# Reordered front of a convolution and MLP kernel: due times, one table half on GpSimd, and index fields as array operations

## The chip, the cores and the metric

The kernel runs on one core of one Trainium2 chip. The metric is the device time of one execution, in microseconds (us). A core has five instruction queues that matter here: TensorE (PE, with its weight loads as PEld), VectorE (DVE), ScalarE (ACT), GpSimd (POOL) and SyncE (SP). Each runs its instructions in program order and waits at semaphores. SP and POOL also issue the DMA transfers, which 16 DMA engines carry out.

## The reference

Inputs are bfloat16, with S = 2048 positions, D = 448 channels and F = 1792 hidden units. `q` is both the input and the residual.

```python
def _A_ref(q, k, v, shift_k, ssm_k, ssm_D):      # q is the layer-normed input
    for t in range(4):                            # four-tap causal filter of k
        k_shift = k_shift + k_pad[:, t:t + S, :] * shift_k[:, 3 - t][None, None, :]
    kv = k_shift * v
    # long causal convolution of kv with ssm_k over S, by FFT of length 2*S
    y = irfft(rfft(kv) * rfft(ssm_k))[:S] + kv * ssm_D
    return q * y

x = A_q
h = x + _A_ref(_layernorm(x), A_k, A_v, A_shift_k, A_ssm_k, A_ssm_D)
# token-mixing MLP on the layer-normed layernorm of h, then a residual
u = gelu(einsum("bsd,sf->bdf", layernorm(layernorm(h)), w1) + b1)
h2 = h + transpose(einsum("bdf,fs->bds", u, w2) + b2)
```

So the work has two halves: a long convolution, done as a discrete Fourier transform of `kv` (called u in the kernel) and of the filter `ssm_k` (called k), and a two-layer MLP across positions.

## The kernel before

**Layout.** Position s = 16 q + r lies in partition q and row r (R = 16 rows of 448 channels).

**The transform** has two stages in each direction. *Stage 1* (`emit_stage1`) multiplies each row r of k or u with two 128 x 128 tables E[2r], E[2r+1] on TensorE into a pair of PSUM banks (L935; for row 0 of k, L939 adds the `ssm_D` term). A *ring copy* (L945) takes the 128 x 896 result to one of eight ring slots in SBUF, and two DMAs (L949) shuffle it into TK (for k) or TU (for u): 112 partitions through POOL's queue, 16 through SP's. Every row goes to partitions that all second-stage products need, so *stage 2* (`emit_stage2`, L966, copies by `evac` at L652 to L656) can begin only when all 16 rows of a branch have landed. Stage 2 uses a small table FW. The *inverse* (`emit_products_i1`) multiplies the two spectra on VectorE (L1017), applies the small tables MA, MN, MB (L1029), copies into TU, and shuffles (L1039) into TZ. `emit_i2` then does the last inverse stage (L1105), the gate (L1112), the residual product (L1119) and the layer norms. The MLP follows (L1200, L1210, L1220, L1224).

**Before stage 1.** The filter is loaded (L810) and transposed on TensorE into KT (`emit_kT`, L916, eight copies by `evac`), between warm-up matmuls (`dummy`, L906). For u, `emit_kv` spreads the four taps over the partitions (WT, four matmuls L870 and four copies), multiplies on VectorE each row's four shifted rows by the taps (L881, 16 times), sums them on TensorE (L887) and multiplies by v (L890, eight times, two rows each). These are the *tap products*. Row r reads rows r to r+3 of KH, whose first three are the *halo* (L822, L824), loaded after the four chunks of k (L818) and of v (L827). The loads of x (L840) and of the first half of w1 (L1175) wait for the last u shuffle; the loads of w2 (L1185) and the second half of w1 (L1178) wait for the last inverse shuffle.

**Tables.** `emit_tables` makes E in two halves of eight rows each: an integer product (L753), an addition (L758) and a mask (L761) per half, then two sines on ScalarE (L766). For FW, MA, MB and MN, integer fields of the partition index are taken into columns of `pc` (L729 to L740, cast at L747), go through POOL (L773, L777), VectorE (L779, masks at L785) and a sine (L781) to POOL's products (L790, L793). `emit_ct` reorders E on POOL (L987, L992) and transposes it into ET (L998).

**The order.** Nothing of the order is written by hand. `op()` records each operation with what it reads and writes, the engine or engines that may do it, an estimated duration, and a due time `sch.t0`. `_Sched.schedule()` is a list scheduler: at each moment it gives a free engine the ready operation with the smallest due time (a longer remaining path breaks ties), and never leaves an engine idle while it has something ready. Readiness goes by the estimates, so the order in which instructions stand in an engine's queue is fixed when the kernel is built. The constants T_... in `_build` are the due times: T_K1 and T_DK1 for stage 1 of k, T_U1 for u, T_KV for the tap products, T_K2 and T_U2 for stage 2, T_TH for the second half of E, T_TN for the fields and small tables, T_CP and T_CT for ET, T_Q and T_DQ for the statistics of x, T_I2 and T_M1 for the end.

An operation with two engines, `FX = ("act", "dve")`, is *flexible*. VectorE takes one only if ScalarE will be busy for at least `flex_slack` ns more, or has at least `flex_back` operations ready:

```python
if (e == "dve" and len(ops[oid].engs) > 1 and
        free_at["act"] - t < self.flex_slack and not self.backlog(ready, ops, started, ready_t, t)):
```

Of the kernel before, what the change touches and what calls it, by code (L numbers as in the profile page):

```python
# [7 lines left out]
ALU = mybir.AluOpType  # L8
# [90 lines left out]
class _Sched:  # L99
# [137 lines left out]

    flex_slack = 200.0
    flex_back = 4

# [269 lines left out]
def _build(nc, A_q, A_k, A_v, A_shift_k, A_ssm_k, A_ssm_D, B_w1, B_b1, B_w2, B_b2, out):  # L510
# [5 lines left out]
    Bsz, S, D = A_q.shape  # L516
# [10 lines left out]
    i32 = DT.int32  # L527
# [38 lines left out]
    with ctx:  # L566
        sch = _Sched(nc, ctx, n_dma_sems=112, small_off=SMALL)
        op = sch.op
# [4 lines left out]
        def view(off, shape, dtype=bf16):  # L573
            size = 4 if dtype in (f32, i32) else 2
            n = 1
            for s_ in shape:
                n *= s_
            ap = AR[:, off // 2: off // 2 + n * size // 2]
            if dtype is not bf16:
                ap = ap.bitcast(dtype)  # L580
            if len(shape) == 2:
                ap = ap.rearrange("p (a b) -> p a b", b=shape[1])
            elif len(shape) == 3:
                ap = ap.rearrange("p (a b c) -> p a b c", b=shape[1], c=shape[2])
            return ap
# [32 lines left out]
        def small(nb):  # L618
            o = sm["o"]
            sm["o"] = o + nb  # L620
            assert sm["o"] <= TOT
            return o

        psum = _Pool(8, pairs=True)
# [13 lines left out]
        FX = ("act", "dve")  # L638
        T_KV, T_DKV, T_KT, T_K1, T_DK1, T_U1, T_DU1 = -7.65, 1.291, -30.53, -12.02, 4.106, 22.58, 2.723
        T_K2, T_U2, T_D2, T_CT, T_BIAS, T_I1, T_DI1 = 38.0, 41.07, 0.276, 40.65, 56.3, 33.93, 0.974  # L640
        T_Q, T_DQ, T_I2, T_DI2, T_M1, T_W1 = 63.71, 8.969, 80.2, 0.401, 96.28, 120.92

        T_TH, T_TN = -43.26, 2.34
        T_CP, T_XL, T_WB = 44.55, -25.02, 149.54
        N_WZ, N_WI, N_W0, N_WK = 24, 16, 9, 5
# [15 lines left out]
        def emit_tables():  # L661
# [27 lines left out]
            assert o_gc + 2560 + 4 * NB <= o_TT + 16384  # L689
            sch.t0 = 0.0  # L690
            op("pool", lambda e, W: e.iota(srow, [[1, R]], base=0, channel_multiplier=R), w=[(o_s, 64)])
# [9 lines left out]
            sch.t0 = 1.0  # L701
            sch.t0 = -30.0
            op("pool", lambda e, W: e.iota(idi, [[1, 128]], base=0, channel_multiplier=-1), w=[(o_gc + 1024, 512)],
               n=128, kind="iota")
            sch.t0 = 1.0
            op("pool", lambda e, W: e.iota(pc[:, 0:1], [[0, 1]], base=0, channel_multiplier=1), w=[(o_p, 4)])
            op("pool", lambda e, W: e.iota(gcol, [[0, 8], [512, 16]], base=0, channel_multiplier=0), w=[(o_gc, 512)],
# [19 lines left out]

            def ints(dst, src, a, b=None):
                op("dve", lambda e, W: e.tensor_scalar(  # L729
                    out=pc[:, dst:dst + 1], in0=pc[:, src:src + 1], scalar1=a[1], scalar2=b[1] if b else None,  # L730
                    op0=a[0], **({"op1": b[0]} if b else {})), r=[(o_p + 4 * src, 4)], w=[(o_p + 4 * dst, 4)], n=1)
            SHR, SHL, AND = ALU.logical_shift_right, ALU.logical_shift_left, ALU.bitwise_and

            sch.t0 = T_TN
            ints(1, 0, (SHR, 6))
            ints(2, 0, (AND, 32), (SHR, 4))
            ints(3, 0, (AND, 3), (SHL, 2))
            op("dve", lambda e, W: e.tensor_tensor(out=pc[:, 1:2], in0=pc[:, 1:2], in1=pc[:, 2:3], op=ALU.bitwise_or),
               r=[(o_p + 4, 8)], w=[(o_p + 4, 4)], n=1)
            op("dve", lambda e, W: e.tensor_tensor(out=pc[:, 4:5], in0=pc[:, 1:2], in1=pc[:, 3:4], op=ALU.bitwise_or),  # L740
               r=[(o_p + 4, 12)], w=[(o_p + 16, 4)], n=1)
            ints(5, 0, (AND, 16), (SHL, 7))
            ints(6, 0, (SHR, 2), (AND, 3))
            ints(7, 0, (AND, 15))
            ints(8, 0, (AND, 15))
            ints(9, 0, (SHR, 4), (AND, 3))
            op("dve", lambda e, W: e.tensor_copy(out=pcf[:, 0:6], in_=pc[:, 4:10]), r=[(o_p + 16, 24)],  # L747
               w=[(o_p + 48, 24)], n=6)
            for h in range(2):
                sch.t0 = T_TH if h else -40.0  # L750
                o_ph = (o_pi, o_X)[h]
                ph = view(o_ph, [16, 128], i32)
                op("dve", lambda e, W, h=h, ph=ph: e.tensor_tensor(  # L753
                    out=ph[:, :, 64:128].rearrange("p (r x) f -> p r x f", x=2),
                    in0=frow.rearrange("p (x f) -> p x f", x=2).unsqueeze(1).broadcast_to([128, 8, 2, 64]),
                    in1=srow[:, 8 * h:8 * h + 8].unsqueeze(2).unsqueeze(3).broadcast_to([128, 8, 2, 64]), op=ALU.mult),
                   r=[(o_fr, 512), (o_s, 64)], w=[(o_ph, 8192)], n=HALF, kind="1x")
                op("dve", lambda e, W, ph=ph: e.tensor_scalar(  # L758
                    out=ph[:, :, 0:64], in0=ph[:, :, 64:128], scalar1=2048, scalar2=None, op0=ALU.add),
# [105 lines left out]
        def emit_kv():  # L865
            sch.t0 = 3.5
            op("pool", lambda e, W: e.memset(ONE, 1.0), w=[(o_one, 256)], n=128)
# [60 lines left out]
        def emit_stage1(src, o_src, T, o_T, tag):  # L928
            for r in range(R):
# [13 lines left out]
                def fn(e, W, b=b, w=w):  # L943
                    dst = WR(w.slots[0])
                    return e.copy(out=dst, in_=Ppair(b)) if W == "act" else e.tensor_copy(out=dst, in_=Ppair(b))  # L945
                op(FX, fn, br=[b], bw=[w], n=2 * D, kind="psum")
                p0 = 64 * (r & 1) + 32 * ((r >> 1) & 1) + (r >> 2)
# [332 lines left out]
```

## Time and profile before

| what | value |
|---|---|
| median of 13 runs | 192.52 us (190.46 to 194.94) |
| the profiled execution | 193.02 us, span 191.2 us |
| PE busy | 175.5 us, 92% of the span |
| DVE busy | 112.1 us, 59% |
| ACT busy | 96.1 us, 50% |
| POOL busy | 68.8 us, 36% |
| mean granted TensorE clock | 0.973 |
| moved by DMA | 35.42 MB, mean 185 GB/s |

The span runs from the first to the last instruction of the profiled execution. A line of the *timeline* or of the *chain of waits* begins with start and duration in us; engine, line of the kernel, operation and tiles follow; brackets hold how long the engine sat idle before it and what released it. A line of the *groups* gives all instructions of one line and shape: their number after the x, then total busy us and mean ns, then idle time before them. All of SBUF is one tile, `arena`, and all of PSUM is `ps`, so instructions are best told apart by their lines.

### The profile page before, as it was taken

The numbers are of one execution on the slowest core, as the hardware profiler recorded it, in microseconds if no ns is written. First come the engines' busy times: TensorE is split into PE (matmuls) and PEld (weight loads), VectorE is DVE, ScalarE is ACT, GpSimd is POOL, SyncE is SP. The second block draws the span as 40 slices with busy tenths as digits, with TensorE's granted clock in tenths as the row PEclk, the third lists the DMA queues.
The fourth block names the chain that finished last, engine by engine and source line by source line (L and its number), as shares of the span: only waits on it lengthen the run. The fifth ranks groups of instructions, "written<-read, shape, count | busy, mean of one in ns | idle before, by whom it ended". The sixth has DMA issues, their size and how long they took to land.

```text
span 191.2 us, 2813 instructions
## 1 busy us (share of the span) xinstructions
PE 175.5 (92%) x1031; PEld 92.9 (49%) x1031; DVE 112.1 (59%) x185; ACT 96.1 (50%) x141; POOL 68.8 (36%) x162
## 2 busy tenths in 40 slices
PE   7899899988498898899789999999999999999993
PEld 2751444334253333224234444555556777777772
DVE  7781989979779999899788875100000222122221
ACT  3095789697969898981479846171221000000000
POOL 8033796669740024449476786000000000000000
PEclk9995799999969999999999999999999999999999
DMA  5996457998664999866599999300000011111111
GB/s 159 409 418 243 139 162 207 221 241 201 154 181 120 392 385 369 275 202 205 159 416 420 419 407 405 111 0 0 0 0 3 8 40 48 48 51 48 48 48 48
DMA packets 15723, 35.42 MB, mean 185 GB/s; under 512 B 3869, under 2 KB 9886, under 8 KB 15710
## 3 DMA queue, kind: packets, MB, share of 16 engines
q1 hardware_dynamic: 11102, 25.59, 35.9%
q0 software_dynamic: 4608, 9.66, 18.2%
q8 instruction: 8, 0.13, 0.3%
q14 instruction: 5, 0.04, 0.1%
HBM read 22.37 MB, written 1.84 MB: 127 GB/s over the span
## 4 chain that ended last, share of the span: by engine, by line
PE 68%; ACT 12%; DMA 9%; DVE 4%; POOL 3%; issue 2%; SPq 1%; ACTq 0%; POOLq 0%
PE ps L1220 22%; PE ps L1210 11%; PE ps L1200 10%; DMA arena<-arena 6%; ACT arena L652 5%; PE ps L966 4%; ACT arena L945 4%; PE ps L1105 4%; PE ps L1029 4%; PE ps L935 3%; DMA arena<-in_A_ssm_k_dram 3%; PE ps L887 2%; ACT arena L1112 2%; PE ps L916 2%; DVE arena L1017 2%
## 5 line engine op out<-in xcount | busy, mean ns | idle before, releaser
L1224 DVE SCALAR_TENSOR_TENSOR arena<-ps,arena 128x448 bf16<-128x448 f32 x16 | 10.9, 684 | 57.3 <-PE ps L1220 57.3
L1220 PE MATMUL ps<-arena 128*128 128x448 bf16 x224 | 42.5, 352 | 0.0
L1220 PEld LDWEIGHTS ps<-arena 128*128 128x128 bf16 x224 | 32.3, 144 | 10.1
L945 ACT CAST arena<-ps 128x896 bf16<-128x896 f32 x29 | 24.9, 914 | 6.5 <-PE ps L939 2.0
L652 ACT CAST arena<-ps 128x896 bf16<-128x896 f32 (+2 forms) x32 | 24.9, 862 | 1.7 <-PE ps L966 0.9
L1200 PE MATMUL ps<-arena 128*128 128x448 bf16 x112 | 23.0, 352 | 0.0
L949 POOL DMA_DIRECT2D arena<-arena x32 | 19.2, 601 | 8.5 <-ACT arena L945 6.6
L1210 PE MATMUL ps<-arena 128*128 128x448 bf16 x112 | 21.4, 352 | 0.0
L935 PE MATMUL ps<-arena 128*128 128x448 bf16 x64 | 17.7, 388 | 1.7 <-DVE arena L890 0.8
L1190 ACT ACTIVATE arena<-ps,arena 128x448 bf16<-128x448 f32 x14 | 8.2, 639 | 20.2 <-PE ps L1210 14.7
L966 PE MATMUL ps<-arena 128*64 128x448 bf16 x128 | 15.9, 390 | 2.6 <-POOL arena L992 1.6
L881 DVE TENSOR_TENSOR arena<-arena 128x1792 bf16<-128x1792 bf16 x16 | 17.9, 1161 | 0.0
L1039 POOL DMA_DIRECT2D arena<-arena x16 | 9.4, 593 | 23.3 <-ACT arena L652 23.1
L1112 ACT ACTIVATE arena<-ps,arena 128x448 f32<-128x448 f32 x16 | 11.5, 723 | 11.2 <-PE ps L1105 8.4
L1017 DVE TENSOR_TENSOR arena<-arena 128x1792 bf16<-128x1792 bf16 x16 | 16.4, 1085 | 0.0
L1029 PE MATMUL ps<-arena 64*128 64x448 bf16 x128 | 14.2, 352 | 2.4 <-ACT arena L652 1.5
L887 PE MATMUL ps<-arena 128*128 128x448 bf16 x64 | 14.4, 353 | 1.8 <-ACT arena L945 1.7
L1200 PEld LDWEIGHTS ps<-arena 128*128 128x128 bf16 x112 | 10.9, 98 | 10.2 <-DVE arena L1160 0.2
L1210 PEld LDWEIGHTS ps<-arena 128*128 128x128 bf16 x112 | 11.0, 98 | 10.2
L1119 DVE SCALAR_TENSOR_TENSOR arena<-arena 128x448 f32<-128x448 bf16 x16 | 10.8, 681 | 4.6 <-ACT arena L1112 4.3
L966 PEld LDWEIGHTS ps<-arena 128*64 128x64 f16 x128 | 6.9, 117 | 11.1 <-ACT arena L652 2.8
L1105 PE MATMUL ps<-arena 128*128 128x448 bf16 x32 | 8.7, 357 | 2.1 <-DMA arena<-arena 1.4
(85 smaller groups left out, 193.9 us busy)
## 6 DMA issues: line engine op xcount, KB each, us to landing
arena<-arena POOLq DMA_DIRECT2D x48, 196.0 KB, 5.2
arena<-in_B_w_dram SPq DMA_DIRECT2D x8, 896.0 KB, 14.1
arena<-in_B_w_dram SPq DMA_DIRECT2D x2, 2048.0 KB, 9.9
arena<-in_B_w_dram SPq DMA_DIRECT2D x2, 1536.0 KB, 17.7
arena<-in_A_k_dram SPq DMA_DIRECT2D x4, 448.0 KB, 8.4
arena<-in_A_v_dram SPq DMA_DIRECT2D x4, 448.0 KB, 9.0
arena<-in_A_q_dram SPq DMA_DIRECT2D x4, 448.0 KB, 4.7
out_dram<-arena SPq DMA_DIRECT2D x7, 224.0 KB, 1.9
```

Source lines behind the costliest of these rows:

```text
L652: return e.copy(out=dst(), in_=src())
L881: op("dve", lambda e, W, T=T, i=i, r=r: e.tensor_tensor(out=T[:, i], in0=KH[:, r:r + 4, :], in1=WT, op=ALU.mult), r=[(o_KH + r * DB, 4 * D ...
L887: op("pe", lambda e, W, b=b, T=T, i=i, j=j: e.matmul(Pb(b, i), ID, T[:, i, j, :], start=(j == 0), stop=(j == 3)), r=[(o_ID, 256), (o + (i ...
L935: op("pe", lambda e, W, b=b, r=r, h=h, dl=dl: e.matmul(Pb(b, h), E[:, 2 * r + h, :], src[:, r, :], start=True, stop=not dl), r=[r_E(r), (o ...
L945: return e.copy(out=dst, in_=Ppair(b)) if W == "act" else e.tensor_copy(out=dst, in_=Ppair(b))
L949: shuf[tag + q_ + str(r)] = shuf[tag + q_] = op(q_, lambda e, W, w=w, p0=p0, a=a, b_=b_, j0=j0: e.dma_start(T[p0:p0 + 29:4, j0:j0 + (b_ - ...
L966: op("pe", lambda e, W, b=bs[h], h=h, j=j, c=c, par=par: e.matmul(PS[64 * par:64 * par + 64, b.slots[c], 0:D], FW[:, 64 * c:64 * c + 64], ...
L1017: op("dve", lambda e, W, m=m, i=i: e.tensor_tensor(out=MR(m.slots[0]).rearrange("p (x y) d -> p x y d", x=2), in0=TU[:, i].unsqueeze(2).br ...
L1029: k = op("pe", lambda e, W, b=bs[h], m=ms[h], par=par, t=t, tab=tab, xy=xy, P=P: e.matmul(Pb(b, par), tab[P, :], MR(m.slots[0])[P, xy, :], ...
L1200: op("pe", lambda e, W, r=r, fc=fc, b=bs[fc]: e.matmul(Pb(b), W1A[:, r, 128 * fc:128 * fc + 128], Q[:, r, :], start=(r == 0), stop=(r == R ...
L1210: op("pe", lambda e, W, r=r, fc=fc, b=b: e.matmul(Pb(b), W1B[:, r, 128 * (fc - n0):128 * (fc - n0) + 128], Q[:, r, :], start=(r == 0), sto ...
L1220: op("pe", lambda e, W, r=r, fc=fc, b=b: e.matmul(Pb(b), W2[fc // 7][:, fc % 7, r:S:R], G[:, fc, :], start=(fc == 0), stop=(fc == NFC - 1) ...
```

## The change

- Due times: stage 1 of k goes from -12.02 + 4.106 r to -39.56 + 0.55 r, the tap products from -7.65 to -37.75, stage 1 of u from 22.58 to 0, stage 2 of u from 41.07 to 9.62 and of k from 38.0 to 29.29 (u now before k), the inverse's products from 33.93 to 12.82, the small tables from 2.34 to -30, and others as the diff shows.
- Ring copies of stage 1 (L945) may go to ScalarE only.
- The product and the addition of E's second half go to POOL; its mask stays on VectorE.
- The fields of the partition index are taken by one array shift, one array AND and two ORs, on a ramp with step 128, with shift counts and masks that 16 POOL memsets write.
- `flex_slack` goes from 200 to 600 and `flex_back` from 4 to 2.

```diff
-    flex_slack = 200.0
-    flex_back = 4
+    flex_slack = 600.0
+    flex_back = 2
...
-        T_KV, T_DKV, T_KT, T_K1, T_DK1, T_U1, T_DU1 = -7.65, 1.291, -30.53, -12.02, 4.106, 22.58, 2.723
-        T_K2, T_U2, T_D2, T_CT, T_BIAS, T_I1, T_DI1 = 38.0, 41.07, 0.276, 40.65, 56.3, 33.93, 0.974
-        T_Q, T_DQ, T_I2, T_DI2, T_M1, T_W1 = 63.71, 8.969, 80.2, 0.401, 96.28, 120.92
-
-        T_TH, T_TN = -43.26, 2.34
-        T_CP, T_XL, T_WB = 44.55, -25.02, 149.54
+        T_KV, T_DKV, T_KT, T_K1, T_DK1, T_U1, T_DU1 = -37.75, 0.96, -43.81, -39.56, 0.55, 0.0, 0.9
+        T_K2, T_U2, T_D2, T_CT, T_BIAS, T_I1, T_DI1 = 29.29, 9.62, 1.375, 22.37, 56.3, 12.82, 0.974
+        T_Q, T_DQ, T_I2, T_DI2, T_M1, T_W1 = 83.98, 17.938, 85.76, 0.401, 91.84, 122.45
+
+        T_TH, T_TN = -38.0, -30.0
+        T_CP, T_XL, T_WB = 20.0, -37.92, 154.44
...
-            sch.t0 = 0.0
+            sch.t0 = -70.0
             op("pool", lambda e, W: e.iota(srow, [[1, R]], base=0, channel_multiplier=R), w=[(o_s, 64)])
...
-            sch.t0 = -30.0
+            sch.t0 = -69.0
             op("pool", lambda e, W: e.iota(idi, [[1, 128]], base=0, channel_multiplier=-1), w=[(o_gc + 1024, 512)],
...
-            op("pool", lambda e, W: e.iota(pc[:, 0:1], [[0, 1]], base=0, channel_multiplier=1), w=[(o_p, 4)])
+            op("pool", lambda e, W: e.iota(pc[:, 0:1], [[0, 1]], base=0, channel_multiplier=128), w=[(o_p, 4)])
...
             sch.t0 = T_TN
-            ints(1, 0, (SHR, 6))
-            ints(2, 0, (AND, 32), (SHR, 4))
-            ints(3, 0, (AND, 3), (SHL, 2))
...
-            ints(9, 0, (SHR, 4), (AND, 3))
+            fields = ((5, 12), (0, 2048), (9, 3), (7, 15), (7, 15), (11, 3), (13, 1), (11, 2))
+            o_fd = small(64)
+            fd = view(o_fd, [16], i32)
+            for i, (sh, mk) in enumerate(fields):
+                op("pool", lambda e, W, i=i, sh=sh: e.memset(fd[:, i:i + 1], sh), w=[(o_fd + 4 * i, 4)], est=120.0)
+                op("pool", lambda e, W, i=i, mk=mk: e.memset(fd[:, 8 + i:9 + i], mk), w=[(o_fd + 32 + 4 * i, 4)], est=120.0)
+            op("dve", lambda e, W: e.tensor_tensor(out=pc[:, 4:12], in0=pc[:, 0:1].broadcast_to([128, 8]), in1=fd[:, 0:8],
+                                                   op=ALU.logical_shift_right),
+               r=[(o_p, 4), (o_fd, 32)], w=[(o_p + 16, 32)], n=8)
+            op("dve", lambda e, W: e.tensor_tensor(out=pc[:, 4:12], in0=pc[:, 4:12], in1=fd[:, 8:16], op=ALU.bitwise_and),
+               r=[(o_p + 16, 32), (o_fd + 32, 32)], w=[(o_p + 16, 32)], n=8)
+            for i in (10, 11):
+                op("dve", lambda e, W, i=i: e.tensor_tensor(out=pc[:, 4:5], in0=pc[:, 4:5], in1=pc[:, i:i + 1],
+                                                            op=ALU.bitwise_or),
+                   r=[(o_p + 16, 4), (o_p + 4 * i, 4)], w=[(o_p + 16, 4)], n=1)
...
-                op("dve", lambda e, W, h=h, ph=ph: e.tensor_tensor(
+                op(("dve", "pool")[h], lambda e, W, h=h, ph=ph: e.tensor_tensor(
                     out=ph[:, :, 64:128].rearrange("p (r x) f -> p r x f", x=2),
...
-                op("dve", lambda e, W, ph=ph: e.tensor_scalar(
+                op(("dve", "pool")[h], lambda e, W, ph=ph: e.tensor_scalar(
                     out=ph[:, :, 0:64], in0=ph[:, :, 64:128], scalar1=2048, scalar2=None, op0=ALU.add),
...
         def emit_kv():
-            sch.t0 = 3.5
+            sch.t0 = -39.0
             op("pool", lambda e, W: e.memset(ONE, 1.0), w=[(o_one, 256)], n=128)
...
-                op(FX, fn, br=[b], bw=[w], n=2 * D, kind="psum")
+                op("act", fn, br=[b], bw=[w], n=2 * D, kind="psum")
```

More of the change, by code (lines that the diff above doesn't have):

```diff
@@ L726, in emit_tables @@
             op("dve", lambda e, W: e.tensor_copy(out=IH, in_=ID), r=[(o_ID, 256)], w=[(o_IH, 256)], n=128)
[L728 to L732, printed above, removed]
@@ L734, in emit_tables @@
-            sch.t0 = T_TN
-            ints(1, 0, (SHR, 6))
-            ints(2, 0, (AND, 32), (SHR, 4))
-            ints(3, 0, (AND, 3), (SHL, 2))
[L738 to L745, printed above, removed]
-            ints(9, 0, (SHR, 4), (AND, 3))
+            sch.t0 = T_TN
+            fields = ((5, 12), (0, 2048), (9, 3), (7, 15), (7, 15), (11, 3), (13, 1), (11, 2))
[4 more added lines that the diff above has]
+                op("pool", lambda e, W, i=i, mk=mk: e.memset(fd[:, 8 + i:9 + i], mk), w=[(o_fd + 32 + 4 * i, 4)], est=120.0)
```

## The prediction

> **What bounds the kernel now.** I read the page first, then the chain of waits, the timeline of the first 100 us, the table by stage, and the groups. All times below are those of the profiled execution: span 191.2 us, 193.0 us with what lies around it, against a median of 192.5 us over the runs shown.
>
> On the page, the 40 slices (4.78 us each) show VectorE and ScalarE at seven to nine tenths from the third slice to about the eighteenth, and the DMA engines full at the start and in the middle but not around slices 5 to 7 and 12.
>
> ```profile
> DVE  7781989979779999899788875100000222122221
> ACT  3095789697969898981479846171221000000000
> ...
> DMA  5996457998664999866599999300000011111111
> ```
>
> The chain of waits shows where the long front part begins and ends: the first ring copy of stage 1 on ScalarE at 17.86, and the last inverse shuffle landing at 88.03 + 3.98 = 92.0.
>
> ```profile
> 17.86 0.91 ACT arena L945
> ...
> 88.03 3.98 DMA arena<-arena
> ```
>
> What follows 92.0 is 32 shuffled-row products, and 448 MLP matmuls at 0.189 us = 84.8 us, on a TensorE that is busy 25.16 of 25.25 us from 99.50 on. The diff moves nothing there, so the change is worth what it takes off 92.0.
>
> ```profile
> 17.86:49.40 31.54, 28.05 (x145) 12.24 (x144) 28.27 (x31) 27.07 (x34) 23.26 (x41) 0.94 0.74 190
> 49.40:62.70 13.30, 10.85 (x86) 5.49 (x88) 10.42 (x10) 10.64 (x13) 5.46 (x13) 0.87 0.52 153
> 62.70:86.80 24.10, 21.27 (x191) 7.58 (x186) 23.35 (x28) 22.71 (x27) 8.51 (x16) 1.00 0.92 319
> ```
>
> This table by stage (columns: window, length, busy PE, PEld, DVE, ACT, POOL, clock, DMA share, GB/s) splits the front. In 62.70:86.80 VectorE and ScalarE are both full: only less work or an earlier start helps. In 49.40:62.70 each idles about 2.8 us and the DMA engines run at half: this stretch is waiting. The timeline tells for what.
>
> ```profile
> 18.72 1.09 DVE L945 CAST arena<-ps 128x896 bf16<-128x896 f32 x1 [3.83 <-PE ps L935]
> ...
> 19.80 4.09 DVE L881 TENSOR_TENSOR arena<-arena 128x1792 bf16<-128x1792 bf16 x4
> ...
> 48.29 1.09 DVE L890 TENSOR_TENSOR arena<-ps,arena 128x896 bf16<-128x896 f32 x1
> ...
> 52.01 4.90 PE L966 MATMUL ps<-arena 128*64 128x448 bf16 x32 [1.64 <-POOL arena L992]
> ...
> 59.54 1.78 SPq L840 DMA_DIRECT2D arena<-in_A_q_dram  x4
> ```
>
> VectorE stands 3.83 us before a ring copy, then does the tap products (L881, L890) from 19.80 to 49.38. The rows of the u branch exist only as these end. The second stage of k starts at 52.01; the load at 59.54 waits for the last u shuffle, so only then can the second stage of u begin.
>
> **The change, part by part.** *Tables.* VectorE loses one 1024-element product (L753, 1.22 us) and one addition (L758, 0.69 us); its mask L761 (1.22 us) stays. GpSimd gets the two. Its rows are far smaller:
>
> ```profile
> L753 DVE TENSOR_TENSOR arena<-arena 128x1024 int32<-128x1024 int32 x2 | 2.4, 1223 | 0.1
> ...
> L777 POOL TENSOR_TENSOR arena<-arena 128x384 int32<-128x384 int32 x1 | 1.0, 1008 | 0.0
> ```
>
> From L777 and L790 (128 elements, 446 ns) the slope is 562/256 = 2.2 ns an element, so the product costs 446 + 896 x 2.2 = 2.4 us. The addition: L773 took 362 ns twice for 128 elements against 252 ns for two (L1076), so 0.9 ns an element and 1.1 us; the upper end is 2.4 us, as if it cost what the product does. Behind the index ramps (about 1 us from 0.8) the pair ends near 5.5 to 7, and the mask by 8.2. VectorE's next work, the kT copies, began at 9.59, and ScalarE's at 9.46 once the last transposes came: the pair is hidden, by at least 1.3 us. The first half gets ahead of the second, so its sine (1.94 + 0.2 us, now at 10.26 behind a kT copy) can run before 9.5.
>
> Here a row speaks against the move. Two L881 beside GpSimd copies took 2.79 us at 42.12 instead of 2 x 1.08, the two copies L992 1.37 instead of 2 x 0.33, and the third L773 1.457 us instead of 0.362. The Trainium skill, "SBUF — State Buffer", section "SBUF: two separate sides", says that VectorE and GpSimd hold a shared port pair exclusively for a whole instruction and the other blocks. By that rule the moved pair and the first half's three operations would run in turn, 3.1 + 3.5 us from 1.9, ending at 8.5 and the mask at 9.7, an estimate that costs 0.2 us; without it, 0.
>
> *Index fields.* Eleven small VectorE operations (0.146 to 0.160 us) become four; the cast stays. That is 1.0 us less on an engine that stood idle there (14.9 to 18.7): nothing by itself. Sixteen GpSimd memsets of 0.09 us, started 0.03 us apart (L697, L698), are 0.5 to 1.4 us in its idle time before 12.5.
>
> *First k row.* Its due time now precedes the last two transpose groups and the four tap broadcasts (L870, 1.74 us), which stood before it on TensorE. First kT copy ended 10.37; the warm-up matmuls (2.05 us) remain; the first row's matmuls took 15.07 to 17.84. I put its ScalarE copy at 13.8, 4 us earlier (2 to 5). Then 32 copies at 0.87 = 27.8 us, plus 2 us of sine and casts: ScalarE could end stage 1 at 43.6.
>
> *Tap products.* The broadcasts, due at -39 instead of 3.5, no longer have their last cast at 18.66 behind a k copy, and no ring copy stands before L881 on VectorE. VectorE still has seven or so kT copies (0.62) and two casts from 9.6, which ends at 15 to 17; I take 16.5, a gain of 3.3. The loads allow it: the k chunks were issued at 3.6 to 6.5 and landed 6.5 to 10.4 us later, all by 16.9. Only the halo rows land at 7.5 + 11.7 = 19.2. They will be later, since the k shuffles now share the DMA engines with the loads (share 0.97 at 9.46:17.86); the first chunk stands in VectorE's queue for them: 0 to 4 us, I take 1.5. The products need 16 x 1.084 + 8 x 1.088 = 26.1 us; GpSimd beside them costs another 1 (0 to 2). Their end: 16.5 + 26.1 + 2.5 = 45.1, instead of 49.4: 4.3 earlier.
>
> *Queues.* SP's small shuffle parts go into the queue behind loads landing until 19.7, so ring slots (eight) come free from about 20; eight copies from 13.8 end at 20.8, so this costs at most 1 to 2 us, on ScalarE. By DMA alone: shares 0.78 and 0.97 up to 17.86, then 0.74 x 31.5 + 0.48 x 10.1 = 28 us of full-rate work; starting 4 us earlier with the 0.89 seen at 30 to 50, it ends at 13.8 + (28 + 4)/0.89 = 50. By the products: 45.1 + 0.9 + 0.9 + 5.2 (median landing) = 52.1. So u is complete at 52, not 59.5.
>
> *Second stages.* k is complete by about 35, so its second stage waits only for the small table. That chain ran from L779 (46.85), behind the last tap product but one, to 50.92. Moved with the products it allows matmuls at 47.7 and a first copy near 49 instead of 53.47. From there to the last inverse copy were 33.4 us, with both engines short; I keep 33. The end: 82.0 instead of 86.84, 4.8 less. The flexible-copy constants (200 to 600 ns, 4 to 2) shift copies between engines 0.91 and 1.09 us apart: 1 us either way.
>
> *Rest.* The statistics' due times spread, but VectorE idles for them from 84.8 to 93 while the shuffles land; without that cover their 12.4 us would show. The W1B load stays tied to the last inverse shuffle, 2.3 us ahead of its use (122.4 against 124.75). Both move along.
>
> Sum: 193.0 - 4.8 = 188.2 on the profiled execution, 187.7 on the median's scale; I say 187.5.
>
> **The rivals.** *More is hidden (0.20).* If the small table gets done in gaps of the products, the 16 second-stage copies of k also fill ScalarE's 4 idle microseconds there, and no halo stall comes: 8 to 10 us less, 183.5. For it: VectorE and ScalarE idled 3.3 and 4.5 us in 17.86:49.40. Against: the products have the earlier due times.
>
> *The small table comes late (0.16).* The fields' due time, -30, lies behind the last product's, -31.03; before, they ran in the gap at 14.05. If that gap closes, everything runs after the products: 0.8 + 3 x 0.73 + 1.0 + 0.56 + 0.63 + 0.45 = 5.6 us plus handovers of about 1. Second-stage matmuls come at 45.1 + 6.6 = 51.7 against 52.0, the gain is 0 to 2, and the time 191. Against it: the broadcasts' transit on TensorE should leave VectorE a microsecond.
>
> *Slower: GpSimd's half holds VectorE (0.14).* The mask stands in VectorE's queue before the kT copies. Each microsecond after 8.2 that the pair ends delays kT, k and the taps alike. From 8.2 + 4.8 = 13 on it decides. If both operations are blocked like the third L773 (1457/362 = 4.0 times), 3.5 us become 14, ending at 15.9: 2.9 us slower, 192.5 + 2.9 = 195.4.
>
> **How the numbers follow.** The forecast has 0.50, at 187.5, with 185 to 190.5 from first tap product, halo and constants. With the rivals, 182 to 193 leaves out the slow tail and the far end of the gain. What 0.5% means is 1 us, about what a measurement here can tell from no change. Faster: 0.50 + 0.20 + half of 0.16 = 0.78; same 0.07; slower 0.15.
>
> **What would show it.** Right: first L945 before 15, first L881 near 16.5, last L890 near 45, the L840 issue near 52, first L653/L656 near 49, TensorE unchanged in the last 99 us. Wrong: kT copies after 10.5 with VectorE waiting for GpSimd before its mask; a wait before L881 for the k load; L773 after the last L890; L966 still at 52.

## The result: 193.5 us, 0.9% slower

The changed kernel took 193.49 us in the median of 11 runs (191.61 to 195.16), beside 192.5 us for the kernel before on the same chips. The ratio is 1.0086, 95% interval 1.0054 to 1.0118: slower, where 187.5 was forecast. Some executions of a kernel, the profiled one of the kernel before among them, are slower whatever the kernel, and the ratios leave these out. So effects are given by ratios (1% is 1.9 us), and a profile, which shows one execution, is used for where time lies. The profiled execution of the changed kernel took 193.64 us, with a span of 191.4.

In the changed kernel the line numbers from the tables on are two less than before (L881 is L879, L945 is L943). In the experiments that mark the two GpSimd operations they are up to seven more than that (the mask L759 is L763, the ring copy L943 is L950).

This table holds the steps that the prediction named, in us from the start of each profiled execution. The last two columns are experiments told of below: the half of the table back on VectorE (e1), and that with 30 warm-up matmuls (e12).

| step | before | predicted | after | e1 | e12 |
|---|---|---|---|---|---|
| first ring copy | 17.86 | 13.8 | 14.71 | 12.53 | 12.26 |
| second tap product starts | 20.80 | - | 22.16 | 19.53 | 20.23 |
| last tap product ends | 49.38 | 45.1 | 50.49 | 47.57 | 47.68 |
| u landed | 59.52 | 52 | 56.68 | 53.74 | 53.83 |
| last inverse copy ends | 86.84 | 82.0 | 84.12 | 81.21 | 81.31 |
| last inverse row landed | 92.02 | - | 90.57 | 87.52 | 87.70 |
| first MLP matmul | 98.55 | - | 98.39 | 95.42 | 94.23 |
| end of the span | 191.18 | - | 191.40 | 188.43 | 187.23 |

Read down the column "after": the first ring copy came early, the tap products ended late, u landed early all the same, and of 2.7 us still in hand at the last inverse copy nothing was left at the end. So the change lost its gain in three places.

**The front.** On the page (busy tenths in 40 slices of 4.79 us) VectorE's fifth and sixth slices, 19 to 29 us, hold 6 and 7 where they held 9 and 8: the tap products do not stream yet. The granted TensorE clock (PEclk) has a new dip in the twentieth slice.

```profile
DVE  8885679988799999995668975100000222122221
...
PEclk9997599999999999999699999999999999999999
```

In the kernel before the clock line was this:

```profile
PEclk9995799999969999999999999999999999999999
```

The chain that ended last (start, length, what) begins with GpSimd's half, which the prediction had off the path:

```profile
4.53 3.47 POOL arena L756
8.02 2.76 DVE arena L759
10.80 1.79 ACT arena L764
12.59 0.80 ACT arena L652
...
85.05 5.52 DMA arena<-arena
```

The addition on GpSimd (L756), the mask on VectorE behind it (L759), the sine on ScalarE (L764), and only then ScalarE's kT copies (L652), which the first row of k needs. In the timeline (brackets: idle time before, and what ended it) the mask took 2.75 us beside a GpSimd memset, where its twin for the first half took 1.21:

```profile
8.02 2.75 DVE L759 TENSOR_SCALAR arena<-arena 128x2048 int32<-128x2048 int32 x1 [0.93 <-POOL arena L756]
8.48 1.21 POOL L813 MEMSET arena<- 1x1344 bf16 x1
```

**The tap products.** VectorE did one at 17.49 and then two kT copies, each waiting for transposes that stand on TensorE behind broadcasts and the first k rows. The stream began at 22.16, later than the 20.80 of before. TensorE's granted clock was 0.50 from 16.3 to 23.1, over the whole of this wait (in the kernel before from 14.6 to 21.5, in e1 and e12 for 3.4 us only), so part of the wait is the clock's; no run separates that part.

```profile
17.49 1.17 DVE L879 TENSOR_TENSOR arena<-arena 128x1792 bf16<-128x1792 bf16 x1
19.53 0.62 DVE L655 COPY arena<-ps 128x896 bf16<-128x896 bf16 x1 [0.87 <-PE ps L914]
21.33 0.62 DVE L655 COPY arena<-ps 128x896 bf16<-128x896 bf16 x1 [1.18 <-PE ps L914]
22.16 3.08 DVE L879 TENSOR_TENSOR arena<-arena 128x1792 bf16<-128x1792 bf16 x3
```

**The stages** (window, length, busy PE, PEld, DVE, ACT, POOL, clock, DMA share, GB/s):

```profile
14.71:50.49 35.78, 34.55 (x169) 14.25 (x168) 28.96 (x34) 31.01 (x40) 28.21 (x49) 0.90 0.71 205
50.49:56.68 6.19, 5.49 (x52) 2.72 (x52) 5.22 (x7) 5.61 (x7) 5.10 (x17) 1.00 0.49 149
56.68:84.12 27.44, 24.79 (x224) 9.38 (x222) 26.60 (x33) 25.99 (x32) 8.31 (x15) 1.00 0.88 304
```

From u's landing to the last inverse copy it is 27.44 us, as before (59.52 to 86.84 is 27.3): VectorE is busy 97% of it. From the last tap product to u's landing it is 6.19 instead of 10.14, and that is where the 2.84 us at u come from. GpSimd's queue in the kernel before shows why: no shuffle was issued between 47.05 and 51.88, because the small table's products (L790, L793) and the reordering of E (L987, L992) stood in front, and then five went out in a row.

```profile
47.05 0.98 POOL L987 COPY arena<-arena 128x256 f16<-128x256 f16 x2
49.10 1.27 POOL L790 TENSOR_TENSOR arena<-arena 128x128 f16<-128x128 f32 x3 [1.07 <-ACT arena L781]
...
51.88 2.98 POOL L949 DMA_DIRECT2D arena<-arena  x5
```

**The end.** The warm-up matmuls (L1047) ended at 87.95, TensorE stood idle for 2.67 us, and from 91.4 ran for 3.4 us at half clock: five matmuls took 2.05 us, where the kernel before has 1.12.

```profile
90.62 0.95 PE L1103 MATMUL ps<-arena 128*128 128x448 bf16 x4 [2.67 <-DMA arena<-arena]
91.63 2.05 PE L1047 MATMUL ps<-arena 128*128 128x448 f16 x5
```

### The profile page after: what moved, and what is told of

Same layout as the page of the kernel before. It is cut to its first block, busy times and chain, and to the rows that moved or that the text cites. A ratio compares the mean times of both kernels' runs of the same rounds, so it can differ in the third digit from the quotient of the medians.

```text
span 191.4 us, 2820 instructions
## 1 busy us (share of the span) xinstructions
PE 176.7 (92%) x1031; PEld 92.6 (48%) x1031; DVE 109.9 (57%) x176; ACT 97.5 (51%) x142; POOL 76.8 (40%) x180
## 4 chain that ended last, share of the span: by engine, by line
PE 67%; ACT 11%; POOL 7%; DVE 7%; DMA 6%; issue 1%; POOLq 0%
PE ps L1218 22%; PE ps L1208 11%; PE ps L1198 10%; DMA arena<-arena 6%; ACT arena L652 5%; PE ps L1103 4%; PE ps L933 4%; PE ps L1027 4%; PE ps L885 4%; PE ps L964 3%; ACT arena L653 2%; POOL arena L947 2%; ACT arena L1110 2%; POOL arena L756 2%; PE ps L1047 2%
## 5 line engine op out<-in xcount | busy, mean ns | idle before, releaser
L1218 PEld LDWEIGHTS ps<-arena 128*128 128x128 bf16 x224 | 32.3, 144 | 10.1
L943 ACT CAST arena<-ps 128x896 bf16<-128x896 f32 x32 | 26.9, 928 | 2.5 <-PE ps L933 2.0
L652 ACT CAST arena<-ps 128x896 bf16<-128x896 f32 (+1 forms) x27 | 22.1, 935 | 1.9 <-PE ps L964 1.1
L1208 PE MATMUL ps<-arena 128*128 128x448 bf16 x112 | 21.3, 352 | 0.0
L879 DVE TENSOR_TENSOR arena<-arena 128x1792 bf16<-128x1792 bf16 x16 | 17.5, 1131 | 0.0
L1037 POOL DMA_DIRECT2D arena<-arena x16 | 9.4, 592 | 19.4 <-DVE arena L655 10.8
L1015 DVE TENSOR_TENSOR arena<-arena 128x1792 bf16<-128x1792 bf16 x16 | 16.5, 1085 | 0.2 <-ACT arena L653 0.2
L1208 PEld LDWEIGHTS ps<-arena 128*128 128x128 bf16 x112 | 11.0, 98 | 10.2
L1117 DVE SCALAR_TENSOR_TENSOR arena<-arena 128x448 f32<-128x448 bf16 x16 | 10.8, 686 | 8.3 <-ACT arena L1110 8.3
L933 PEld LDWEIGHTS ps<-arena 128*128 128x128 f16 x64 | 5.9, 106 | 12.5 <-ACT arena L652 2.8
```

The costliest lines, as they stand in the source:

```text
L652: return e.copy(out=dst(), in_=src())
L879: op("dve", lambda e, W, T=T, i=i, r=r: e.tensor_tensor(out=T[:, i], in0=KH[:, r:r + 4, :], in1=WT, op=ALU.mult), r=[(o_KH + r * DB, 4 * D ...
L933: op("pe", lambda e, W, b=b, r=r, h=h, dl=dl: e.matmul(Pb(b, h), E[:, 2 * r + h, :], src[:, r, :], start=True, stop=not dl), r=[r_E(r), (o ...
L1208: op("pe", lambda e, W, r=r, fc=fc, b=b: e.matmul(Pb(b), W1B[:, r, 128 * (fc - n0):128 * (fc - n0) + 128], Q[:, r, :], start=(r == 0), sto ...
L1218: op("pe", lambda e, W, r=r, fc=fc, b=b: e.matmul(Pb(b), W2[fc // 7][:, fc % 7, r:S:R], G[:, fc, :], start=(fc == 0), stop=(fc == NFC - 1) ...
```

## The experiments

All ran beside the kernel before on the same chip, and ratios are to that kernel, with 95% intervals. Times are medians of 12 runs, of 6 for e9, e11 and e12. The changed kernel was not run again beside the experiments, so what an experiment gains on it is the difference of the two ratios, which is uncertain by about 1 us.

### GpSimd's half of the table

**e1, the half back on VectorE.** The order of all instructions stays as planned with the two operations on GpSimd; then only their engine is changed (`h1` marks the product and the addition).

```diff
         order = self.schedule()
+        for o in self.ops:
+            if getattr(o, 'tag', '') == 'h1':
+                o.eng = 'dve'
```

> The changed kernel with its order of instructions kept as planned, but the product and the addition of E's second half done by VectorE, at the same places of the order. Theory G (GpSimd's half holds the front): the two operations took 2.64 and 3.46 us on GpSimd, slowed VectorE's neighbours (L724 1.92 us instead of 1.08, L726 1.02 instead of 0.23) and made the mask end at 10.78, so kT copies come 1.1 us and the first row of k (matmul at 13.44) 1.1 to 1.5 us earlier, and the whole time falls by 1 us or more against the changed kernel. Theory T (the last two transpose groups hold the tap products, whatever the start): the start moves the same 1 us, but what follows on TensorE (broadcasts, three rows of k, two transpose groups) keeps its length, 13.44 to 21.3, so the second tap product moves from 22.2 to about 21 and no further. Theory N (only later stages decide): the last tap product moves by 1 us and the time does not.

Measured: 189.99 us, ratio 0.9924 (0.9875 to 0.9973). Undoing this one part turns the loss into a gain, 1.6% or 3.1 us below the changed kernel. The profile has the second mask done at 8.06 instead of 10.77 and ScalarE's kT copies at 9.91 instead of 12.50:

```profile
6.83 1.23 DVE L763 TENSOR_SCALAR arena<-arena 128x2048 int32<-128x2048 int32 x1
9.91 1.69 ACT L655 COPY arena<-ps 128x896 bf16<-128x896 bf16 x2
```

From there the steps are 2.2 to 3.0 us earlier, to the end of the span. Theory G holds, and the size is well above the 1 us that it asked for at least. Theories T and N fall: the second tap product came at 19.53, not at 21, and the time moved. Part of the size can be the clock's, which in this profile was 0.50 from 15.6 to 19.0 only. e10 and e12 below repeat the step on one chip (31 and 30 warm-up matmuls, the half on GpSimd and on VectorE): 1.0001 and 0.985, which is 2.9 us.

**e7, the addition alone back on VectorE.** The mark is on the second operation only.

> The changed kernel in its own order, with the second half's addition alone taken back to VectorE and its product left on GpSimd. Theory A (the addition is the term that was mis-sized: 3.46 us on GpSimd, and the mask behind it): the mask ends near 8 us instead of 10.8, the first kT copies start near 9.4, the first ring copy near 12.6, and the time is that of the run with the whole half on VectorE, 189.5 to 190.7 us. Theory P (any large GpSimd operation beside VectorE's table work costs as much): the product keeps a good part, the mask ends after 9.2, and the time lies between, 191 to 192.5 us.

Measured: 191.60 us, ratio 0.997 (0.993 to 1.001), between e1 and the changed kernel, as theory P has it. The mask ended at 9.65: of its 2.7 us, about 1.1 are the addition's and 1.6 stay with the product, whose 2.63 us on GpSimd hold VectorE's small operations (L727 took 1.92 us, in e1 0.68) and push GpSimd's memsets and ramps into the first mask, which took 2.23 us. The kT copies started at 11.10, though, waiting 1.45 us for TensorE, which in this execution ran at half clock from 8.5 to 11.8, and the first ring copy came at 14.66, no earlier than in the changed kernel; so the split of the time between the two operations is less sure than that of the mask.

**e8, the half on GpSimd in the kernel before.** The same marks in the kernel before, with `'pool'` for `'dve'`.

> The kernel before in its own order, with the product and the addition of the second half alone given to GpSimd. Theory G (the half on GpSimd costs about 3 us wherever it is put): the second mask ends near 10.8 us instead of 8.5, the first kT copies come after 10.6 instead of 9.46, the first ring copy 1.5 to 3 us later than 17.86, and the time is 194 to 195.5 us. Rival (the old order has slack between the kT copies and the tap products, which started at 19.80 behind a halo load that landed at 19.34): the tap products move by less than 0.7 us and the time stays within 0.8 us of 192.5.

Measured: 194.17 us in the median of all runs against 192.59, but the ratio is 1.0015 (0.9966 to 1.0064). So a loss of 194 us or more, 0.8% and up, is not there: theory G falls for the old order, and the time is the rival's. In the profile, of an execution of 195.6 us, the first ring copy and the first tap product came 0.9 us later than before, which is more than the rival allowed and less than G had. So the same half costs about 3 us in the new order, where the front waits for it, and in the old one nothing that these runs can measure. The profile also settles the price of the addition, because VectorE stood idle all the while:

```profile
7.44 2.81 POOL L762 TENSOR_SCALAR arena<-arena 128x1024 int32<-128x1024 int32 x1
10.28 2.49 DVE L765 TENSOR_SCALAR arena<-arena 128x2048 int32<-128x2048 int32 x2 [4.08 <-POOL arena L762]
```

It costs 2.81 us on GpSimd with nobody in the way, 2.7 ns an element, where VectorE needs 0.69. The 3.46 us of the changed kernel are this price and 0.65 more beside VectorE's operations. The Trainium skill, "GPSIMD Engine Reference", section "4.1 Engine selection", has one-input operations on GpSimd at roughly line rate; this row is four times VectorE's, and the row decides.

What VectorE and GpSimd do to each other can be seen in e3 below, which has the same front. There the mask got ahead of the memset of 1344 elements, and the memset stood still:

```profile
8.01 1.66 DVE L759 TENSOR_SCALAR arena<-arena 128x2048 int32<-128x2048 int32 x1 [0.93 <-POOL arena L756]
8.53 2.29 POOL L813 MEMSET arena<- 1x1344 bf16 x1
```

In both profiles the pair is through at 10.8; who comes second differs, by 1.1 us for the mask. That agrees with "SBUF — State Buffer", section "SBUF: two separate sides": the port pair is held for a whole instruction, and the other engine blocks. The page says this of a VectorE operation in a 2-port mode or with two SBUF inputs; the mask has one input, and no run shows its mode.

### The head of the tap products

**e2, the transposes earlier.** Transposes and kT copies are due three units sooner, so that their last two groups come before the broadcasts.

```diff
-        T_KV, T_DKV, T_KT, ... = -37.75, 0.96, -43.81, ...
+        T_KV, T_DKV, T_KT, ... = -37.75, 0.96, -46.81, ...
```

> The changed kernel with the transposes' due time 3 us earlier (T_KT -46.81), so that all eight groups stand ahead of the first row of k on TensorE. Theory T: VectorE no longer stands 0.9 + 1.2 us before two kT copies at 19.5 and 21.3; the second tap product comes at 18 to 19, when the halo rows have landed (17.8), instead of 22.2, and the last one near 47.5 instead of 50.5; the time falls by 2 to 3 us. Theory G: the start of the tap products moves by less than 1 us, since the mask still ends at 10.8. Theory N: last tap product 3 us earlier, time unchanged within 0.5 us, because the later stages take it back.

Measured: 190.77 us, ratio 0.9966 (0.9932 to 1.0), 2.3 us below the changed kernel. The first product started at 18.70, the stream ran on from 19.89, the last product ended at 48.89, 1.6 us earlier, and u landed 1.3 us earlier. But the last inverse copy ended at 84.24, no earlier than the 84.12 of the changed kernel. In this profile the whole gain lies behind it: the last inverse row landed 1.3 us earlier, and there was no half-clock period (TensorE idle for 1.28 us only). So theory T is right on the head of the stream, the time that it forecast came from elsewhere, and up to the last inverse copy it went as theory N had it.

**e5, three edits.** e1, e2, and 44 warm-up matmuls.

> The changed kernel with all three edits that helped alone: the second half's product and addition on VectorE, the last two transpose groups of the filter due at -46.81, 44 warm-up matmuls before the last stage instead of 24. Theory S (three separate losses, which add): -3.5 us, -2.7 us and -1.9 us against 193.5 give 185.4 us, the last tap product ending near 46. Theory H (the first two share one bound, the landing of the halo rows: in the run with the half on VectorE the stream already waited 0.21 us for that load at 19.53): the tap products stream from 18.5 to 19.5 us as in either run alone, end at 47.5 to 48.5, u lands at 53.5 to 54.5, and the time is that of the half on VectorE less the half-clock period near 88 us, 188.0 to 189.5 us.

Measured: 190.50 us, ratio 0.9909 (0.9871 to 0.9947): no better than e1. Theory S falls. The products stream from 19.91, having waited 1.52 us for the halo rows, so e1's and e2's gains share that bound, as theory H says. But the time is not the 188 to 189.5 that H gave: the first MLP matmul came 8.7 us after the last row's landing at 87.19, against 6.53 in the kernel before. 44 warm-up matmuls were too many.

**e6, the halo rows loaded early.** e5 with the loads of the halo behind the first chunk of k and v, not behind all four.

```diff
-                sch.t0 = -10.5
+                sch.t0 = -13.8
```

> The same three edits, and the loads of the halo rows issued before the chunks of k and v (sch.t0 -13.8 instead of -10.5 at the loads of k). Theory H (the halo rows bound the start of the tap products once the queue before them is short): the stream starts near 16.5 to 17.5 us, 1.5 to 2.5 us earlier than with the three edits alone, the last tap product ends near 46, and the time falls by as much, to 186.0 to 187.5 us. Rival (the k chunk itself, the tap broadcasts or v take the halo's place): the stream starts within 0.5 us of the run without this edit and the time stays within 0.7 us of it.

Measured: 193.74 us, ratio 1.0019 (0.9972 to 1.0066). The halo landed at 11.8 and the stream began at 17.51, but the last product ended at 46.84 as in e5, and u landed 2.2 us later than there. In its profile VectorE waits 2.59 us at 22.18 for a sum on TensorE, and the clock is 0.82 from 17 to 30. So the halo bounds the start and not the end of the stream; what bounds the end, and why this kernel is 1.1% or 2.1 us slower than e5, stays open. The clock alone is not it: the four executions with a mean clock of 0.998 and more took 191.1 to 191.9, the two of e5 190.3 and 190.6.

### The cover before the last stage

**e3, 44 warm-up matmuls.** `N_WZ` goes from 24 to 44.

> The changed kernel with 44 instead of 24 warm-up matmuls (N_WZ, L1047) between the last inverse product and the first shuffled-row product; nothing else changes. In the changed kernel TensorE stood idle 87.95 to 90.6 and the granted clock was 0.5 from 91.4 to 94.8, so that five warm-up matmuls took 2.05 us instead of 1.12 while the first rows of the last stage wait for each other. Theory C (clock): TensorE works until the shuffles land, no half-clock period falls behind 85 us, and the time falls by 1.0 to 1.7 us. Rival: the half-clock period has another cause; it stays, and the time is the same or, with 20 matmuls more (3.8 us) in TensorE's queue past the landing, up to 1.2 us longer.

Measured: 191.61 us, ratio 1.0021 (0.9983 to 1.0059), 1.3 us below the changed kernel, as theory C has it. No half-clock period lies after 85. As in e5 the matmuls outlast the landing: 8.5 us from there to the first MLP matmul. The profile cannot price the edit, because its front was 1.1 us earlier by the mask told of above.

**e10, 31 warm-up matmuls.** The same with 31, and nothing else.

> The changed kernel with 31 warm-up matmuls instead of 24 and nothing else. Theory W: the landing of the last inverse row and the inverse's last matmul stay (90.6 and 83.2), the half-clock period near 91 to 95 goes, the first MLP matmul comes 6.5 us after the landing instead of 7.8, and the time is 191.7 to 192.7 us, 1 to 1.8 less than the changed kernel, which is that of the kernel before. Rival (the half-clock period comes for another reason than TensorE's idle time): it stays, and the time stays within 0.6 us of 193.5.

Measured: 192.0 us, ratio 1.0001 (0.9958 to 1.0044), 0.85% or 1.6 us below the changed kernel. The row landed at 90.37, as in the changed kernel; the idle time is 1.23 us, and five matmuls take 1.12 us instead of 2.05:

```profile
90.42 0.93 PE L1103 MATMUL ps<-arena 128*128 128x448 bf16 x4 [1.23 <-DMA arena<-arena]
91.41 1.12 PE L1047 MATMUL ps<-arena 128*128 128x448 f16 x5
```

Theory W holds. The windows say it in the clock (third number from the end): 0.50 in the changed kernel, which stands first, 1.00 in e10. The other executions agree: by their mean clocks (last section) those of the changed kernel had 2.8 such periods on average, those of e10 1.8.

```profile
91.40:94.80 3.40, 3.34 (x10) 1.34 (x10) 2.58 (x6) 1.48 (x3) 0.22 (x2) 0.50 0.87 265
```

```profile
91.40:94.80 3.40, 3.33 (x17) 1.42 (x17) 3.04 (x7) 2.11 (x4) 0.50 (x1) 1.00 0.95 286
```

### The order of the second stages, and the small table alone

**e4, the second stages' due times of before** (k, u and the inverse's products; the front is the changed kernel's).

```diff
-        T_K2, T_U2, T_D2, ..., T_I1, T_DI1 = 29.29, 9.62, 1.375, ..., 12.82, 0.974
+        T_K2, T_U2, T_D2, ..., T_I1, T_DI1 = 38.0, 41.07, 0.276, ..., 33.93, 0.974
```

> The changed kernel with the due times of the second stages and the inverse products as before (T_K2 38.0, T_U2 41.07, T_D2 0.276, T_I1 33.93): k before u again; the front up to the last tap product is planned the same. Theory O (order of the second stages costs): in the changed kernel the last four copies of k's second stage came at 76.7 to 80.8, products waited for them, and from the last u shuffle to the last inverse copy were 27.4 us although half of k was done before; with k first that stretch falls to 25 to 26 and the time by 1.5 us. Rival: both engines are full in that stretch whatever the order, it stays at 27 to 27.5, and the time is the same within 0.6 us.

Measured: 191.45 us, ratio 0.999 (0.9954 to 1.0026). The stretch from u's landing to the last inverse copy is 28.4 us, not shorter than the 27.4 of the changed kernel, so the new order of the second stages did not lose the gain. The rival holds for that stretch. The time is 1.8 us lower all the same, more than the rival allowed. In the profile the inverse's last matmul comes later, the 24 warm-ups reach closer to the landing (idle 1.48 us), and there is no half-clock period; that this is the whole reason is not shown.

**e11, the small table early in the kernel before.** `T_TN` goes from 2.34 to -30, and nothing else.

> The kernel before with the small tables' due time alone changed, from 2.34 to -30. Theory Q (in the kernel before the last u shuffles stood in GpSimd's queue behind the small table's products, which waited for a sine that came behind the tap products: no shuffle was issued between 47.06 and 51.88, and u landed 10.1 us after the last tap product): the small table is done before 35, the shuffles follow their copies, u lands 6 to 7.5 us after the last tap product, near 56.5, the second stage of k starts before 50, and the time falls by 1.5 to 3 us, to about 190. Rival (the stretch from u's landing to the last inverse copy grows by what is gained, since VectorE and ScalarE are both full there and the small table's 3 us go in front of the tap products): u lands earlier by less than 1.5 us or the stretch of 27.3 us grows, and the time stays within 0.8 us of 192.5.

Measured: 193.25 us, ratio 1.0122 (1.0058 to 1.0187), slower. In its profile (of its slowest execution, 195.47 us) the tail from the last tap product to u's landing is 7.9 instead of 10.1 us, so the queue does play the part that theory Q gave it, but five shuffles still went out together at 52.52, behind the reordering of E. And the second tap product started at 23.51 instead of 20.80. Theory Q's gain is not there. The rival's account, that the front pays what the tail gains, fits, but 2.3 us slower is outside the 0.8 that it allowed. And not all of the late front need be the table's: VectorE's first kT copy came at 10.98 instead of 9.59, waiting for TensorE, and of the table's work only the index fields stood in front of it on VectorE. What made it late stays open.

### Together

**e12 and e9.** e1 with 30 warm-up matmuls, and that with e2's transposes.

> The half on VectorE and 30 warm-up matmuls, the transposes as in the changed kernel. Theory W: the half-clock period at 87.3 to 90.7 of the run with the half on VectorE alone goes, the first MLP matmul comes 6.5 us after the last row's landing instead of 7.9, and the time is 1 to 1.5 us below that run's 190.0, at 188.5 to 189. Theory H (the transposes' order and the half share one bound): it stands within 0.6 us of the run that also has the transposes first. If the two add after all, it is 1 to 2 us slower than that one.

> The half on VectorE, the transposes first, and 30 warm-up matmuls before the last stage (24 in the changed kernel, 44 in the run with three repairs). Theory W (the warm-ups must just cover the stretch from the inverse's last matmul to the last shuffled row: with 44 of them at about 0.19 us the first MLP matmul came 8.7 us after that landing instead of 6.5, with 24 TensorE stood idle and ran at half clock): the first MLP matmul comes 6.4 to 6.8 us after the landing near 87.2, no half-clock period lies after 85, the span ends near 186.5 and the time is 188 to 189 us, 1.5 to 2.5 below the run with 44. Rival (the 2 us are not the warm-ups' but the later rows'): the time stays within 0.7 us of 190.5.

Measured: e12 188.56 us, ratio 0.985 (0.981 to 0.989); e9 188.25 us, ratio 0.9838 (0.9789 to 0.9887). Both beat both kernels. The two repairs of e12 add: 3.1 us from e1 and 1.6 from e10 make 4.7, and e12 is 4.5 below the changed kernel. The transposes add 0.2 more, within the noise, not 2.3: theory H. Theory W holds in both: the first MLP matmul came 6.5 us after the landing. What is left at the head is the halo load, in e12:

```profile
20.23 3.31 DVE L886 TENSOR_TENSOR arena<-arena 128x1792 bf16<-128x1792 bf16 x3 [1.19 <-DMA arena<-in_A_k_dram]
```

## Why the prediction was wrong

It was 6.0 us too low. Two of its terms, set at nothing, cost 3.1 and 1.6 us; with both put right (e12) the kernel gains 1.5%, 2.9 of the 5.0 us that were forecast. Of the 2 us that are left, 1.2 lie in the profiles between the last inverse copy and the landing of its row: 6.39 us in e12, 5.18 in the kernel before. The last shuffle took 5.46 us there instead of 3.98, and why stays open. The ring copies on ScalarE alone, the constants for flexible copies and the index fields were not tried by themselves.

**Tables: the term that failed most.** The prediction priced the pair on GpSimd at 2.4 + 1.1 us and called it hidden by 1.3 us at least. The product's 2.64 fits. The addition's 1.1 was 3.46 in place and 2.81 by itself; even the upper end, 2.4, was below. The slope came from operations of 2 and 128 elements, and the third L773, at four times its siblings, was read as blocking only. Worse, the mask was taken at its price on a free VectorE, 1.2 us, and cost 2.75, blocked by GpSimd's memset and ramps; the page's rule was applied to the moved pair and not to what GpSimd does next. So the mask ended at 10.77 instead of 8.2, VectorE's kT copies started at 10.69, and the sign that the prediction gave for being wrong (after 10.5, with VectorE waiting for GpSimd before its mask) was met. And the cover was read from the old order. The prediction took ScalarE's first kT copy, at 9.46, as work that the mask had only to precede; that copy stood ahead of the sines then. Now ScalarE's two kT copies stand behind the sine that waits for the mask, and came at 12.50. That path, mask, sine, copies, first row, is what e1 shortens by 2.2 us at the first ring copy.

**The rival on GpSimd's half** named the right place and a wrong price. It let nothing be lost until the pair ends after 8.2, and decide from 13 on. The pair ended at 8.0 and the loss was 3 us.

**Rest: "both move along".** This was the second failing step. The last inverse row landed only 1.45 us earlier although the last copy was 2.7 earlier (the last shuffle took 5.52 us instead of 3.98), and the fixed 24 warm-up matmuls, which had ended 1.39 us before the landing, now ended 2.67 before it. TensorE went to half clock for 3.4 us just where nothing hides it. "TensorE unchanged in the last 99 us" was refuted by 1.6 us: from the landing to L1208 it is 34.2 us, before 32.6.

**Tap products.** The start at 16.5 left two kT copies out of VectorE's queue and held the halo for a stall of the first chunk alone. In fact the first product did start at 17.49 but the stream at 22.16, and in e2, e5 and e12 at 19.9 to 20.2, in the last two when the halo rows landed. The length was about right: 26.1 + 2.5 is 27.5 without the first product, and from the second on it was 26.7 us in e5, 27.5 in e12 and 28.3 in the changed kernel.

**What held.** The first ring copy came 3 us earlier (5 in e1). The small table was done early, in the gap that the prediction trusted. k's second stage had its first matmul at 40.93 and its first copy at 44.06, where the latter was forecast near 49. u's landing gained, though by GpSimd's clear queue rather than by earlier products, which the prediction did not see. The stretch behind it kept its length, and the last inverse copy of e12, at 81.31, is near the 82.0 that was worked out. That nearness is partly luck: u landed 1.8 us later than forecast there, and the stretch behind it took 27.5 us where the forecast left 30.

## What to carry to other kernels

Price a moved operation on its new engine from a row of the same kind and size, then follow its result through every engine that waits for it, and price its neighbours beside it, not alone. When an edit shifts the work around a fixed run of warm-up matmuls, count again how long TensorE stands idle behind them. Gains at the head of a stream add only up to its latest input: ask of each what the stream would wait for next.

## What the runs showed of the hardware

- Ahead of the last stage, TensorE's granted clock was 0.50 for 3.4 us with 2.67 us (the changed kernel) and 2.53 us (e1) without a matmul; with 1.48 us or less, in seven other profiles, it was not. In between, 2.03 us (e7) left the clock alone and 1.73 us (e8) was followed by such a period, as was 1.64 us at 52.01 in the kernel before, so no sharp limit can be read from these runs.
- At the front the clock was 0.50 for 6.8 us in the kernel before, the changed kernel, e2, e4, e6, e8, e10 and e11, for 3.4 us in e1, e3, e7, e9 and e12, and not at all in e5. Idle time cannot be the whole reason: in the kernel before and in e1 TensorE is shown busy without a break from 9.5 until the clock fell at 14.6 and 15.6. The reason is open.
- One period of 3.4 us at half clock takes 0.009 off the mean clock of a span of 191 us, so an execution's mean clock counts its periods. In the changed kernel five executions with 0.981 or 0.982 (two periods) took 191.6 to 192.8 us, four with 0.973 (three) 193.4 to 193.6, three with 0.965 (four) 194.9 to 195.2. In e10 five with 0.991 (one) took 191.1 to 191.4, five with 0.980 or 0.982 191.9 to 192.4, two with 0.973 193.0. In the kernel before and in e6 the times of one clock spread more widely.
- Which of VectorE and GpSimd goes first can change with nothing changed in the front: the same mask took 2.75 us in the changed kernel, e2, e4 and e10, and 1.66 in e3, and that is 1.1 us at the kT copies.
